# One 2048-column transposing DMA for q and k of a token block in the first chunk, and scores held behind the first gate/up step

## The chip, the cores and the metric

The kernel runs on one core of a Trainium2 chip. The metric is the device time of one execution in microseconds (us). The kernel before took 567.59 us, the median of three runs between 567.03 and 569.25 us. All views of the profile come from one profiled execution.

## The reference

The input x has 2048 tokens of 576 numbers, in bf16. The output is x plus the product of a windowed attention and a gated feed-forward block, both on the normalised x:

```
xn = layernorm(x)
q, k, v = split(xn @ wqkv)                 # 32 heads of 18 numbers
p = softmax(q k^T / sqrt(18), masked to the last 256 tokens)
s = (p v) @ wo
h = sigmoid(xn @ w_gate) * (xn @ w_up)     # 4608 columns each
out = x + s * silu(h @ w_down)
```

## The kernel before

**Tiles and stages.** The tokens are worked in four chunks of 512 (CH), each of four blocks of 128 (P). A chunk goes through the layernorm, q, k and v for each block (line 465), the attention, the gate and up products (line 810, called f below), the down product (line 930, called f2) and the output projection (line 740). The contraction over 576 is cut in nine pieces of 64 rows. In f, rows 0 to 63 of the TensorE array work on gate and rows 64 to 127 on up, so two matmuls of 64x512 run side by side; one tile of 128 columns (ft, 36 in a chunk) takes nine such pairs, 18 matmuls.

**An order written by a planner.** Every piece of work is an Op with an engine, a cost, dependencies and a priority. The function schedule() books them by start time on five in-order queues (PE, ACT, DVE, POOL, and SP for all DMAs), and emit() writes the queues out with semaphore waits. So the order on each queue is fixed when the kernel is built; on the chip, an instruction whose input is late holds all that stands behind it on its queue. DMAs are booked with an issue cost on SP, and with bytes on one shared transfer line of 320 bytes/ns.

**q and k.** For the scores, q and k must lie with their head rows on partitions. build_qk() copies the projection of one block out of PSUM into a buffer of 32 heads padded to 32 columns (1024 columns), q by DVE and k by ACT, and one transposing DMA (line 213, issued at 518) moves it to qkp. Chunk 0 issues eight of these: the first three from the ring pk, the other five from the first half of the five slots of expr, which the attention later uses for the exponentials. In qkp a head group holds 512 columns of q, 512 of k, and 256 of the keys that the chunk before left (the tail, copied by POOL at 641). In chunk 0 the eight DMAs are kept behind the weights of the third group of f (QKT_BEHIND, line 859).

**Scores.** build_unit() makes a unit: 16 or 24 small matmuls (line 594) into PSUM banks 0 to 3, two exponentials on ACT (612), masks on DVE (630). Four units serve a pair of head groups, and build_pv() (663) follows. Chunk 0 has 16 units. Units are put between steps of f, which is the filler; f uses banks 4 to 7, and its tiles end with a tanh on ACT (824) and a multiply on DVE (828).

**Weights of f.** Three tiles share a group of weights (fg), loaded by four DMAs into a ring of three slots (RW). Group 3 takes the slot of group 0, so its loads can start when tile 2 has been worked, and it is needed by tile 9.

**The exchange at XS.** Until tile XS[c], gate and up of a tile end in the same pair. At that tile two pieces of gate are worked in the upper rows, with weights from an extra load (sat, load_x()), and from there gate ends two pairs ahead of up. The last up tile takes the two places back. XS is 10 in chunk 0 and 1 in the others.

Of the kernel before, what the change touches and what calls it, by code (L numbers as in the profile page):

```python
# [4 lines left out]
ACTF = mybir.ActivationFunctionType  # L5
# [5 lines left out]
DH = 18  # L11
F = 4608
P = 128
CH = 512
# [23 lines left out]
RPK = 3  # L38
# [2 lines left out]
NOT = 4  # L41
WO_PRIO = 1
KL = 4 * DH
RS = 4
RXF = 2
RTH = 2
RREC = 2
RBN = 4
XS = (10, 1, 1, 1)
XP = (4, 0)  # L50
RUN = 3
WX_PRIO = -1
# [20 lines left out]
DMA_ISSUE_NS = 440.0  # L73
W_ISSUE_NS = 660.0
XT_ISSUE_NS = 1300.0
OC_SLACK = 3000.0
LATE_SLACK = 5000.0
LN_STEP = 1
XT_CUT = 4
QKT_BEHIND = {2: 0}  # L80
WARM = 10
X0_SLACK = 0.0
# [4 lines left out]
W_FACTOR = 1.42  # L87
X0_FACTOR = 1.7
XT_BYTES = 1.2
XT0_BYTES = 1.5  # L90
W0_FACTOR = 1.5
DMA_LAT_NS = 1600.0
DMA_BYTES_PER_NS = 320.0
# [80 lines left out]
class Builder:  # L174
# [141 lines left out]
    def build_init(self):  # L316
# [23 lines left out]
        self.op_pkz.append(op("ACT", 2500, lambda e: e.memzero(self.expr[:, :, 0:2, :]), "pkz2", prio=0))  # L340

    def warm(self, n, name, deps):
        ps = Psum((3,))
# [141 lines left out]
            "p t (h d) -> p t h d", d=DH)  # L485

    def build_qkv(self, c):
        self.op_q, self.op_k, self.op_qkt = [], [], []
        old = [o for l in self.op_sc[c - 1] for o in l] + self.op_tail if c > 0 else []
        order = QKV_FIRST if c == 0 else QKV_NEXT  # L490
        prev = None
        for w in order.split():
            i, j = int(w[1]), "qkv".index(w[0])
            o = (self.build_v if j == 2 else self.build_qk)(c, i, j, old)
            if c > 0:
                o.odeps += ([prev] if prev and QKV_CHAIN else []) + (self.op_xn[QKV_GATE] if not prev else []) + ([self.f2_ops[QKV_F2]] if QKV_F2 else [])
                o.prio = QKV_PRIO
            prev = o

    def build_qk(self, c, i, j, old):  # L500
        extra = len(self.op_qkt) - RPK if c == 0 else -1
        if extra < 0:
            spk, dpk = self.r_pk.take()
            pk = self.pk[:, spk, :, :]
        else:
            dpk = []
            pk = self.expr[:, extra, 0:2, :].rearrange("p a (h d) -> p (a h) d", d=HP)
        o, ps = self.project(c, i, j, f"qk:{c}:{i}:{j}", dpk, self.op_pv[c - 1][NHG - 1] if c > 0 else None)

        def f_ev(e):  # L510
            dst = pk[:, :, 0:DH].rearrange("p (t h) d -> p t h d", t=2)
            if j == 0:
                return e.tensor_copy(dst, self.halves(ps))  # L513
            return e.activation(dst, self.halves(ps), ACTF.Copy)
# [6 lines left out]
        if extra < 0:  # L521
            self.r_pk.release(spk, dm)
        else:
            self.r_exp.release(extra, dm)
        (self.op_q, self.op_k)[j].append(dm)
        self.op_qkt.append(dm)
        return o

# [49 lines left out]
    def build_unit(self, c, u, low, up, masks):  # L578
# [5 lines left out]
        def f_sc(e):  # L584
            for _, k in slots:
                for j in range(4):
                    r0 = 32 * j
                    for half, pieces in enumerate((low, up)):
                        if k >= len(pieces):
                            continue  # L590
                        hg, kb, q0, n, pos = pieces[k]
                        b = ps.banks[j] * 512 + pos * 64
                        k0 = CH + kb * 64 if kb >= 0 else 2 * CH + (kb + 4) * 64
                        r = e.matmul(self.ps[64 * half:64 * half + 64, b:b + n * 64],  # L594
                                     self.qkp[r0:r0 + DH, hg, k0:k0 + 64],
                                     self.qkp[r0:r0 + DH, hg, q0 * 64:(q0 + n) * 64],
                                     start=True, stop=True, tile_position=(r0, 64 * half))
            return r
# [174 lines left out]
    def build_ffn(self, c):  # L773
# [67 lines left out]
        for n0, n1 in zip(cuts, cuts[1:]):  # L841
# [60 lines left out]
            for key in done:  # L902
# [342 lines left out]
```

## Time and profile before

| what | value |
|---|---|
| median of three runs | 567.59 us (567.03 to 569.25) |
| the profiled execution, device time | 567.65 us |
| its span in the trace | 565.0 us |
| mean granted TensorE clock | 0.999 of full |
| TensorE matmul busy | 555.0 us (98%) |
| ACT busy / DVE busy | 274.6 us (49%) / 307.4 us (54%) |
| bytes moved by DMA | 73.29 MB, mean 130 GB/s |

The span runs from the first to the last instruction; the device time is 2.65 us longer. A busy TensorE (PE) is one with a matmul under way; the ends of matmuls are modelled. In the views, "x16" is a count of instructions merged in a row, the number in brackets is the idle time ahead of the first of them with what ended it, and "SPq" is the DMA-issuing queue. A wait for several semaphores is put down to the one that came last by the profile; where the engine named cannot be the cause, it was another, often a DMA.

### The profile page before, as it was taken

How to read it: one execution, taken by the hardware profiler on the slowest of the kernel's cores; microseconds unless marked ns; L12 is line 12 of the kernel's file. 1: busy time of each engine (PE TensorE's matmuls, PEld its weight loads, DVE VectorE, ACT ScalarE, POOL GpSimd, SP SyncE). 2: the span in 40 equal slices, each digit the busy share in tenths (PEclk: the TensorE clock that was granted, in tenths of full speed). 3: DMA queues.
4: the chain of work that ended last, by engine and by line, in shares of the span. 5: the costliest groups of instructions: out<-in, count | busy, mean ns of one | idle time of the engine just before them, and what ended most of it. 6: DMA issues, size and time to landing. Idle time of an engine off the chain costs nothing.

```text
span 565.0 us, 17870 instructions
## 1 busy us (share of the span) xinstructions
PE 555.0 (98%) x7830; PEld 283.0 (50%) x7854; DVE 307.4 (54%) x664; ACT 274.6 (49%) x372; POOL 28.2 (5%) x55
## 2 busy tenths in 40 slices
PE   8999999999999999999999999999999999999997
PEld 5634444457544444456654444445665444444544
DVE  6136987741136886772204778767121586686213
ACT  7456665514146947721407576580220855855011
POOL 3000001010000100010000011001000000000100
PEclk9999999999999999999999999999999999999999
DMA  8999999628956665324794665713559355660001
GB/s 200 219 187 249 231 224 215 136 62 114 181 105 148 151 151 135 86 52 83 106 210 109 144 153 122 161 36 71 89 124 206 87 126 129 147 131 23 20 22 43
DMA packets 126026, 73.29 MB, mean 130 GB/s; under 512 B 54782, under 2 KB 125438, under 8 KB 125950
## 3 DMA queue, kind: packets, MB, share of 16 engines
q1 hardware_dynamic: 125950, 72.16, 62.0%
q8 instruction: 62, 1.02, 0.8%
q14 instruction: 14, 0.11, 0.1%
HBM read 55.48 MB, written 2.36 MB: 102 GB/s over the span
## 4 chain that ended last, share of the span: by engine, by line
PE 94%; SPq 2%; DMA 1%; issue 1%; DVE 1%; ACT 0%
PE ps L810 50%; PE ps L930 23%; PE ps L465 8%; PE ps L594 5%; PE ps L663 4%; PE ps L740 3%; SPq L214 2%; PE ps L960 2%; DMA wqkv_sb<-in_A_wqkv_dram 1%; ACT sat L755 0%; ACT expr L612 0%; DVE tf L679 0%; DVE hT L828 0%; DVE pk L681 0%; DVE tf L684 0%
## 5 line engine op out<-in xcount | busy, mean ns | idle before, releaser
L810 PE MATMUL ps<-xn,wgs 64*128 64x512 bf16 x2576 | 296.3, 377 | 1.4 <-ACT expr L612 1.4
L810 PEld LDWEIGHTS ps<-xn,wgs 64*128 64x128 bf16 x2576 | 119.4, 94 | 143.7 <-issue 8.9
L612 ACT ACTIVATE expr<-ps 128x1024 bf16<-128x1024 f32 x152 | 147.2, 1022 | 26.3 <-PE ps L594 26.1
L930 PE MATMUL ps<-wd_sb,hT 128*128 128x64 bf16 (+1 forms) x1056 | 131.0, 284 | 2.2 <-issue 1.0
L824 ACT ACTIVATE tring<-ps 128x512 bf16<-128x512 f32 x144 | 86.3, 600 | 82.8 <-PE ps L810 80.6
L828 DVE SCALAR_TENSOR_TENSOR hT<-tring,ps 128x512 bf16<-128x512 bf16 x144 | 97.9, 680 | 30.6 <-ACT tring L824 14.2
L930 PEld LDWEIGHTS ps<-wd_sb,hT 128*128 128x128 bf16 x1080 | 68.1, 98 | 65.0 <-issue 1.4
L630 DVE TENSOR_TENSOR expr<-expr,m 128x512 bf16<-128x512 bf16 (+2 forms) x152 | 58.5, 412 | 55.5 <-ACT expr L612 54.5
L991 ACT ACTIVATE thf<-ps 128x576 bf16<-128x576 f32 (+2 forms) x17 | 10.6, 622 | 135.5 <-PE ps L930 128.3
L993 DVE SCALAR_TENSOR_TENSOR thf<-thf,ps 128x576 bf16<-128x576 bf16 (+2 forms) x17 | 12.2, 719 | 106.5 <-ACT thf L991 106.5
L465 PE MATMUL ps<-wqkv_sb,xn 64*128 64x288 bf16 x864 | 54.7, 283 | 0.5 <-ACT xn L454 0.2
L465 PEld LDWEIGHTS ps<-wqkv_sb,xn 64*128 64x128 bf16 x864 | 42.9, 94 | 11.2 <-issue 1.8
L594 PEld LDWEIGHTS ps<-qkp 18*64 18x64 bf16 x1472 | 16.2, 103 | 32.6 <-ACT expr L612 14.0
L594 PE MATMUL ps<-qkp 18*64 18x320 bf16 (+4 forms) x1472 | 32.4, 259 | 0.1
L641 POOL COPY qkp<-qkp 128x256 bf16<-128x256 bf16 x24 | 9.8, 410 | 288.1 <-PE ps L594 288.1
L513 DVE CAST pk<-ps 128x576 bf16<-128x576 f32 x15 | 11.3, 755 | 23.1 <-PE ps L465 22.9
L703 DVE STREAM_TRANSPOSE op__63<-pk 128x512 bf16<-128x512 bf16 x32 | 22.3, 698 | 0.2
L663 PEld LDWEIGHTS ps<-expr,vau 64*32 64x32 bf16 x1440 | 18.0, 92 | 7.6 <-issue 4.9
L681 DVE STREAM_TRANSPOSE pk<-ps 128x512 f32<-128x512 f32 x32 | 21.5, 673 | 0.0
L663 PE MATMUL ps<-expr,vau 64*32 64x320 bf16 (+5 forms) x1440 | 20.9, 253 | 0.3
L740 PE MATMUL ps<-wo_sb,oT 64*128 64x512 bf16 (+1 forms) x288 | 18.7, 283 | 0.1
L679 DVE STREAM_TRANSPOSE tf<-ps 128x512 f32<-128x512 f32 x16 | 11.5, 716 | 11.8 <-PE ps L663 11.8
(54 smaller groups left out, 197.1 us busy)
## 6 DMA issues: line engine op xcount, KB each, us to landing
wgs<-in_B_w_gate_dram SPq DMA_DIRECT2D x48, 240.0 KB, 3.9
wgs<-in_B_w_up_dram SPq DMA_DIRECT2D x48, 240.0 KB, 4.9
wgs<-in_B_w_up_dram SPq DMA_DIRECT2D x48, 192.0 KB, 4.0
wgs<-in_B_w_gate_dram SPq DMA_DIRECT2D x48, 192.0 KB, 4.8
wd_sb<-in_B_w_down_dram SPq DMA_DIRECT2D x9, 576.0 KB, 8.2
xf<-in_A_x_dram SPq DMA_DIRECT2D x18, 144.0 KB, 2.2
out_dram<-xf SPq DMA_DIRECT2D x15, 144.0 KB, 2.0
xr<-in_A_x_dram SPq DMA_DIRECT2D x14, 144.0 KB, 4.7
```

The costliest lines, as they stand in the source:

```text
L465: r = e.matmul(self.bank(ps, HV, hf), self.xn[r0:r0 + 64, k, i * P:(i + 1) * P], self.wqkv_sb[r0:r0 + 64, j, k, :], start=(k == 0), stop=( ...
L594: r = e.matmul(self.ps[64 * half:64 * half + 64, b:b + n * 64], self.qkp[r0:r0 + DH, hg, k0:k0 + 64], self.qkp[r0:r0 + DH, hg, q0 * 64:(q0 ...
L612: return e.activation(self.expr[:, es, 2 * pr:2 * pr + 2, :], src, ACTF.Exp, scale=SM_SCALE)
L630: return e.tensor_tensor(ap, ap, m, ALU.mult)
L663: r = e.matmul(self.ps[32 * j:32 * j + 32, b + q0 * 64:b + (q0 + n) * 64], vf[:, v0:v0 + 32], self.expr[p0:p0 + 64, es, j, pos * 64:(pos + ...
L681: t3 = self.rd("DVE", dve_ns(CH), lambda e, tg=tg, hg=hg: e.transpose(tg, self.bank(ps2[hg][1])), f"t3:{c}:{hg}", deps=[o, self.last_mul] ...
L703: t2 = self.op("DVE", dve_ns(CH), lambda e, on=on: e.transpose(self.op_[:, hg % NOT, :], on.rearrange("p g d -> p (g d)")), f"t2:{c}:{hg}" ...
L740: r = e.matmul(self.bank(ps2[w], n1 - n0, n), self.oT[r0:r0 + 64, kt, qi * P:(qi + 1) * P], self.wo_sb[r0:r0 + 64, kt, n0:n1], start=(swap ...
L810: return e.matmul(self.bank((pg, pu)[gu][ft]), w, self.xn[r0:r0 + 64, i, :], start=first, stop=last, tile_position=(r0, 0))
L824: return e.activation(self.tring[:, st_, :], self.bank(ps), ACTF.Tanh, scale=0.5)
L828: return e.scalar_tensor_tensor(self.hT[:, ft, :], self.tring[:, st_, :], 1.0, self.bank(ps), ALU.add, ALU.mult)
L930: r = e.matmul(self.ps[:, b + n0:b + n1], lhsT, self.wd_sb[:, q, fl, n0:n1], start=(ft == 0), stop=(ft == NFT - 1))
```

## The change

In chunk 0, q and k of a block are laid side by side in one buffer of 2048 columns (the slots 0 and 1 of pk for block 0, all four rows of the slots 0 to 2 of expr for the others), with the head groups of q and k alternating. One transposing DMA moves both, so there are four instead of eight; each waits for both copies. To let one DMA write both, q and k stand at one stride in qkp (KO = 640 columns): 512 of q and 128 of the tail, then 512 of k and the other 128 of the tail. The addresses of the scores and of the tail copy follow. The memset of expr covers 3 slots whole instead of 5 slots half. Chunks 1 to 3 keep their eight DMAs of 1024 columns, at the new addresses.

The planner's costs change for these DMAs: 1500 ns of issue for 2048 columns (1300 for 1024 before), and a factor of 1.2 on the bytes where it was 1.5. XS of chunk 0 goes from 10 to 13. In chunks 1 to 3 every score unit is ordered behind the first step of f (SC_GATE).

```diff
+KO = CH + P
-XS = (10, 1, 1, 1)
+XS = (13, 1, 1, 1)
+XT0_ISSUE_NS = 1500.0
+SC_GATE = 0
-XT0_BYTES = 1.5
+XT0_BYTES = 1.2
...
-        self.op_pkz.append(op("ACT", 2500, lambda e: e.memzero(self.expr[:, :, 0:2, :]), "pkz2", prio=0))
+        self.op_pkz.append(op("ACT", 2500, lambda e: e.memzero(self.expr[:, 0:3, :, :]), "pkz2", prio=0))
...
     def build_qk(self, c, i, j, old):
-        extra = len(self.op_qkt) - RPK if c == 0 else -1
-        if extra < 0:
+        if c == 0:
+            both = self.pk[:, 0:2, :, :].rearrange("p j h d -> p (j h d)") if i == 0 else \
+                self.expr[:, i - 1, :, :].rearrange("p a c -> p (a c)")
+            pk = both.rearrange("p (t g j h d) -> p t g j h d", t=2, g=4, j=2, d=HP)[:, :, :, j, :, 0:DH]
+            dpk = []
+        else:
             spk, dpk = self.r_pk.take()
             pk = self.pk[:, spk, :, :]
-        else:
-            dpk = []
-            pk = self.expr[:, extra, 0:2, :].rearrange("p a (h d) -> p (a h) d", d=HP)
...
-        c0 = j * CH + i * P
-        dm = self.dma(self.qkp[:, :, c0:c0 + P], pk.rearrange("p h d -> p (h d)"),
-                      (XT_BYTES if c else XT0_BYTES) * 8 * P * P * 2, f"qkt:{c}:{i}:{j}", ("qk", i, j), deps=[ev] + old, prio=0,
-                      issue=XT_ISSUE_NS, transpose=True)
+        if c == 0:
+            if j == 0:
+                self.op_qe.append(ev)
+                return o
+            dst = self.qkp[:, :, :].rearrange("p g (j c) -> p (g j) c", j=2)[:, :, i * P:(i + 1) * P]
+            dm = self.dma(dst, both, 2 * XT0_BYTES * 8 * P * P * 2, f"qkt:{c}:{i}", ("qk", i), deps=[ev, self.op_qe[i]] + old,
+                          prio=0, issue=XT0_ISSUE_NS, transpose=True)
...
+        else:
+            c0 = j * KO + i * P
+            dm = self.dma(self.qkp[:, :, c0:c0 + P], pk.rearrange("p h d -> p (h d)"), XT_BYTES * 8 * P * P * 2,
+                          f"qkt:{c}:{i}:{j}", ("qk", i, j), deps=[ev] + old, prio=0, issue=XT_ISSUE_NS, transpose=True)
...
-                        k0 = CH + kb * 64 if kb >= 0 else 2 * CH + (kb + 4) * 64
+                        k0 = KO + kb * 64 if kb >= 0 else CH + (kb + 4) // 2 * KO + kb % 2 * 64
...
-                    self.qkp[:, hg, 2 * CH:2 * CH + 2 * P], self.qkp[:, hg, 2 * CH - 2 * P:2 * CH]),
+                    self.qkp[:, hg, :].rearrange("p (j c) -> p j c", j=2)[:, :, CH:CH + P],
+                    self.qkp[:, hg, KO + CH - 2 * P:KO + CH].rearrange("p (j c) -> p j c", j=2)),
...
             prev = o
+            if n0 == SC_GATE and c > 0:
+                for l in self.op_sc[c]:
+                    for u in l:
+                        u.odeps.append(o)
```

More of the change, by code (lines that the diff above doesn't have):

```diff
@@ L487, in build_qkv @@
     def build_qkv(self, c):
-        self.op_q, self.op_k, self.op_qkt = [], [], []
+        self.op_q, self.op_k, self.op_qkt, self.op_qe = [], [], [], []
         old = [o for l in self.op_sc[c - 1] for o in l] + self.op_tail if c > 0 else []
@@ L508, in build_qk @@
         o, ps = self.project(c, i, j, f"qk:{c}:{i}:{j}", dpk, self.op_pv[c - 1][NHG - 1] if c > 0 else None)
         def f_ev(e):
-            dst = pk[:, :, 0:DH].rearrange("p (t h) d -> p t h d", t=2)
+            src = self.halves(ps)
+            if c == 0:
+                dst, src = pk, src.rearrange("p t (g h) d -> p t g h d", g=4)
+            else:
+                dst = pk[:, :, 0:DH].rearrange("p (t h) d -> p t h d", t=2)
             if j == 0:
-                return e.tensor_copy(dst, self.halves(ps))
@@ L514, in f_ev @@
-            return e.activation(dst, self.halves(ps), ACTF.Copy)
+                return e.tensor_copy(dst, src)
+            return e.activation(dst, src, ACTF.Copy)
         ev = self.rd("ACT" if j else "DVE", act_ns(D) if j else dve_ns(D), f_ev, f"qke:{c}:{i}:{j}",
                      deps=[o, self.op_pkz] + [t for t in (self.op_on[c - 1] if c > 0 else [])], prio=1, psum=[ps])
-        c0 = j * CH + i * P
-        dm = self.dma(self.qkp[:, :, c0:c0 + P], pk.rearrange("p h d -> p (h d)"),
-                      (XT_BYTES if c else XT0_BYTES) * 8 * P * P * 2, f"qkt:{c}:{i}:{j}", ("qk", i, j), deps=[ev] + old, prio=0,
-                      issue=XT_ISSUE_NS, transpose=True)
@@ L521, in build_qk @@
-        if extra < 0:
+        if c == 0:
+            if j == 0:
[4 more added lines that the diff above has]
+                          prio=0, issue=XT0_ISSUE_NS, transpose=True)
+            if i > 0:
+                self.r_exp.release(i - 1, dm)
+            else:
+                for k in (0, 1):
+                    self.r_pk.rel[k].append(dm)
+            self.op_q.append(dm)
+            self.op_k.append(dm)
+        else:
+            c0 = j * KO + i * P
+            dm = self.dma(self.qkp[:, :, c0:c0 + P], pk.rearrange("p h d -> p (h d)"), XT_BYTES * 8 * P * P * 2,
+                          f"qkt:{c}:{i}:{j}", ("qk", i, j), deps=[ev] + old, prio=0, issue=XT_ISSUE_NS, transpose=True)
@@ L522, in build_qk @@
             self.r_pk.release(spk, dm)
-        else:
-            self.r_exp.release(extra, dm)
-        (self.op_q, self.op_k)[j].append(dm)
+            (self.op_q, self.op_k)[j].append(dm)
         self.op_qkt.append(dm)
```

## The prediction

> **What bounds the kernel now.** I read the page first, then the waits of PE, then PE's, SP's and ACT's timelines of the first 50 us, then the landings of single DMAs, and last the score matmuls by stage.
>
> ```profile
> PE 555.0 (98%) x7830; PEld 283.0 (50%) x7854; DVE 307.4 (54%) x664; ACT 274.6 (49%) x372; POOL 28.2 (5%) x55
> ...
> PE 94%; SPq 2%; DMA 1%; issue 1%; DVE 1%; ACT 0%
> ```
>
> PE has a matmul under way for 555.0 of 565.0 us, and the chain that ended last runs through PE for 94%. The change removes no matmul. So it can win only from the 10 us in which PE stands still, or lose by adding to them. The waits say where these are:
>
> ```profile
> PE ps L347 <- DVE neghalf L318: 1.5, 1, 1.5
> PE ps L810 <- ACT expr L612: 1.4, 1, 1.4
> PE ps L930 <- issue: 1.0, 6, 0.2
> PE ps L444 <- DVE xnr L421: 0.9, 1, 0.9
> ```
>
> The first and fourth are the start, ahead of anything the change touches; the third is six pieces of under 0.2 us. The second is one stall of f, and it lies in chunk 0:
>
> ```profile
> 17.83 1.24 PE L810 MATMUL ps<-xn,wgs 64*128 64x512 bf16 x10
> ...
> 23.70 12.75 PE L810 MATMUL ps<-xn,wgs 64*128 64x512 bf16 x116
> 36.55 0.42 PE L594 MATMUL ps<-qkp 18*64 18x320 bf16 x16
> 36.90 3.19 PE L810 MATMUL ps<-xn,wgs 64*128 64x512 bf16 x28
> 40.03 0.43 PE L594 MATMUL ps<-qkp 18*64 18x64 bf16 x24
> 40.39 1.04 PE L810 MATMUL ps<-xn,wgs 64*128 64x512 bf16 x8
> 42.79 1.04 PE L810 MATMUL ps<-xn,wgs 64*128 64x512 bf16 x8 [1.37 <-ACT expr L612]
> ```
>
> Count the matmuls of f up to the stall: 10 + 116 + 28 + 8 = 162 = 9 x 18. PE stands exactly ahead of tile 9, the first tile of weight group 3. The profile names the exponentials, but f does not read them. So I look for the weights on SP:
>
> ```profile
> 19.67 0.62 SPq L214 DMA_DIRECT2D wgs<-in_B_w_up_dram  x1
> 20.33 7.47 SPq L213 DMA_TRANSPOSE qkp<-pk  x3
> 27.85 7.86 SPq L213 DMA_TRANSPOSE qkp<-expr  x5
> 35.76 0.60 SPq L214 DMA_DIRECT2D wgs<-in_B_w_gate_dram  x1
> 36.40 0.63 SPq L214 DMA_DIRECT2D wgs<-in_B_w_up_dram  x1
> 37.07 0.62 SPq L214 DMA_DIRECT2D wgs<-in_B_w_gate_dram  x1
> 37.73 0.62 SPq L214 DMA_DIRECT2D wgs<-in_B_w_up_dram  x1
> ```
>
> The eight transposing DMAs hold SP from 20.33 to 35.71, and the four loads of group 3 stand behind them. The slot they go to is free much earlier, when tile 2 ends: 54 matmuls, 10 of them done early, so 23.70 + 44 x 12.75/116 = 28.5 us. The last of the four, issued at 37.73, takes this long to land:
>
> ```profile
> L214 SPq DMA_DIRECT2D wgs<-in_B_w_up_dram x1: 616/616/616, 37.7 to 37.7; - x1
> ...
> DMA to landing us min/median/max: 4.7/4.7/4.7
> ```
>
> It lands at 42.4, and PE goes on at 42.79. Could it be a PSUM bank that ACT frees late? ACT's timeline rules that out:
>
> ```profile
> 39.06 0.60 ACT L824 ACTIVATE tring<-ps 128x512 bf16<-128x512 f32 x1
> 40.60 1.94 ACT L612 ACTIVATE expr<-ps 128x1024 bf16<-128x1024 f32 x2 [0.94 <-PE ps L594]
> 42.42 0.60 ACT L824 ACTIVATE tring<-ps 128x512 bf16<-128x512 f32 x1
> ```
>
> Tile 9 takes the banks of tile 7, whose tanh ended at 39.66. The next one, for tile 8, ends at 43.02, after PE had gone on. So the stall is weights late behind the transposing DMAs, and it is worth 1.37 us.
>
> **The change, part by part.**
>
> **The DMAs.** Eight issues become four, of twice the columns. No row shows 2048 columns. Smaller ones are there:
>
> ```profile
> L213 SPq DMA_TRANSPOSE xn<-xnr x24: 1209/1271/2224, 105.8 to 397.6; - x24
> L213 SPq DMA_TRANSPOSE qkp<-pk x27: 1232/1336/3429, 20.3 to 428.7; - x27
> ```
>
> The xn group has 640 and 512 columns (576 in the mean), the qkp group 1024. From 576 to 1024 columns the median grows by 0.065 us; carried on in a straight line, 2048 columns take 1.336 + 0.065 x 1024/448 = 1.48 us (the lower bound). In proportion to the columns they take 2 x 1.336 = 2.67 us (the upper bound). I take 1.5 us, by the nearer pair of rows, which are almost flat.
>
> The Trainium skill speaks against this: "DMA: Bandwidth & Descriptors", in a table of its section "Why a DMA increments its semaphore by 16 and not by 1", gives 262,144 cycles of issue for an SBUF to SBUF transpose of 8,192 tiles on generations before trn3, one push for each tile. By that, twice the columns cost twice the issue, and nothing would be saved; the two rows above do not follow it between 576 and 1024 columns, and it stays as a rival below.
>
> Part of the 15.38 us on SP isn't issue: 8 x 1.34 is 10.7, and the rest, 4.7 us, is blocking, which shows in the first and second DMA:
>
> ```profile
> L213 SPq DMA_TRANSPOSE qkp<-pk x1: 3370/3370/3370, 20.3 to 20.3; - x1
> ...
> DMA to landing us min/median/max: 7.3/7.3/7.3
> ...
> L213 SPq DMA_TRANSPOSE qkp<-pk x1: 2697/2697/2697, 23.8 to 23.8; - x1
> ...
> DMA to landing us min/median/max: 4.7/4.7/4.7
> ...
> L213 SPq DMA_TRANSPOSE qkp<-expr x1: 2282/2282/2282, 33.4 to 33.4; - x1
> ...
> DMA to landing us min/median/max: 4.2/4.2/4.2
> ```
>
> These landed at 27.6, 28.5 and 37.6. The weights ahead of them still fill the DMA engines then, and that stays. What limits the new ones from below is the data: the closest two landings are 0.9 us apart for 1024 columns. From 27.6 for the first 1024 columns the other seven need at least 6.3 us, so the last DMA lands no earlier than 33.9; if nothing is won, at 37.6 as now. SP was free 1.9 us ahead of that landing (35.7), so it will be free between 32.0 and 35.7. My value is about 32.5: four issues of 1.5 are 6 us, so data and the old blocking set the end.
>
> **The wait added.** A block's DMA now waits for q and k. The copies of k come last:
>
> ```profile
> 20.61 0.65 ACT L514 ACTIVATE expr<-ps 128x576 bf16<-128x576 f32 x1 [3.02 <-PE ps L465]
> ...
> 23.92 0.65 ACT L514 ACTIVATE expr<-ps 128x576 bf16<-128x576 f32 x1 [0.45 <-PE ps L465]
> ```
>
> The first is done at 21.26, 0.93 us after SP gets there; all are done at 24.57. Behind the waiting DMA stand the other three and then group 3. This costs nothing while the first DMA would be blocked by the weights until 23.7 anyway; without that cover it is 0.93 us on SP.
>
> **The loads behind.** Group 3 landed 42.4 - 35.7 = 6.7 us after SP came free. So it lands at 39.2 (bounds 38.7 to 42.4). PE needs it at 41.43. The stall is gone if SP is free by 34.7, that is, 1.0 us earlier than now: gain 1.37 us. Later groups follow the same queue and are earlier too.
>
> **The first score.** With 16 matmuls (four pieces for four heads) it is the unit of keys 2 to 5, which needs q and k of blocks 1 to 3, so it waited for the seventh of eight DMAs before (k of block 2) and waits for the last of four now. The planner books 262,144 bytes x 1.5 / 320 = 1.23 us a DMA before, 1.97 us now; seven are 8.6, four 7.9 us. So it places the first score some 0.7 us sooner, near 35.8. The data, at 33.9 to 37.6, may be up to 1.9 us late there; I take zero, as my value of SP free at 32.5 puts the landing at 34.4. Starting attention earlier wins nothing by itself, as f fills PE meanwhile.
>
> **XS from 10 to 13.** Tiles 10 to 12 lose the lead of two pairs (2 x 0.22 us), so their tanh starts 0.2 to 0.4 us later. The cover is the second pair of banks, a whole tile of 2 us. Bounds: nothing, and 0.4 us for each of three tiles where an exponential stands ahead of the tanh, 1.2 us. I take nothing, since the planner sees this wait and puts scores elsewhere.
>
> **Memset, copies, scores, tail.** The memset of expr grows from 5 x 1024 to 3 x 2048 columns, by a fifth:
>
> ```profile
> 3.48 2.32 ACT L340 ACTIVATE expr<-expr 128x2560 uint32<-128x2560 uint32 x1
> 6.48 3.37 ACT L454 ACTIVATE xn<-ps 128x512 bf16<-128x512 bf16 x6 [0.68 <-PE ps L444]
> ```
>
> That is 0.46 us of the 0.68 that ACT waits next; without this cover it would delay the first copy of xn by 0.46. The other instructions keep their sizes.
>
> **SC_GATE.** In chunk 1 the order is so already (columns of the stretches: PE busy with scores and their count, then weight loads):
>
> ```profile
> 124.66:160.20 35.54, 0.00 (x0) 0.00 (x0) 1.00 0.88 149
> 160.20:245.00 84.80, 8.53 (x384) 4.14 (x384) 1.00 0.51 116
> ...
> 160.21 1.25 PE L810 MATMUL ps<-xn,wgs 64*128 64x512 bf16 x9
> ```
>
> No score matmul stands ahead of the first step of f at 160.21. It costs nothing where the order stays.
>
> **Sum.** Span 565.0 - 1.37 = 563.6; with the 2.65 us around the span, 566.3 against 567.65 of the profiled execution. That execution is 0.06 above the median, so **566.2** against 567.59, 0.24% less.
>
> **The rivals.** A measurement of this kernel can tell 0.5% (2.8 us) from no change.
>
> *No gain at the stall.* If the profile is right to name the exponentials, or SP is free only after 34.7 by other work moved up, the time stays at 567.6. For it: the second exponential ends at 42.54, close to 42.79. Against it: the count of 162.
>
> *Issue in proportion to columns.* Four DMAs of 2.67 us with the same blocking: last landing 37.6 as now, group 3 at 42.4. PE stands at the first score from 35.8 to 37.7, 1.9 us, and reaches tile 9 at 43.3, after the weights: 1.9 - 1.4 = +0.5, 568.1. For it: the second and later DMAs of a run (1.336) are slower than the first (1.232), as if each waited for the one ahead. Against it: 576 columns take 1.271. The page's rule of a push for each tile leads here.
>
> *Slower: 2048 columns block SP.* If a DMA of 2048 columns is too much for the queue to take ahead, each blocks as the first did, 3.37 + 1.37 = 4.7 us. Then SP is free at 21.3 + 19 = 40.3, the last DMA lands at 42.2, and the first score holds PE for 6.4 us, less the 1.4 of the old stall: 567.6 + 5.0 = 572.6. It decides from a landing later than 35.8 + 1.4 + 2.8 = 40.0. For it: 3.37 and 2.28 us. Against it: the five in between go at 1.34.
>
> *More than the stall.* The short waits of f2 (1.0) and the one of the first transposes on PE (L444, 0.9) go too: 566.2 - 1.9 = 564.3. Nothing in the change reaches them, but a plan that is made anew may.
>
> **How the numbers follow.** Forecast 0.64, no gain 0.08, proportion 0.16, blocking 0.08, more 0.04. Faster than 564.7 is the last and 0.01 of the forecast's edge: 0.05. Slower than 570.4 is blocking and 0.01 of proportion with the exchange's 1.2 on top: 0.09. The rest, 0.86, lies within 0.5%. The range goes from 565.0 (1.2 under the forecast: the short waits of f2, or twice the 0.56 by which the lowest of the three runs lies under the median) to 568.6 (proportion, with 0.5 of the exchange); it leaves out the last two cases and the edges.
>
> **What would show it.** Right: four transposing DMAs on SP of about 1.5 us plus blocking, the loads of group 3 issued by 34.7, no wait of PE ahead of its matmul 163 of f, a first score without a wait, and PE's other waits as before. Wrong: issues near 2.7 us or more, a PE wait ahead of the first score matmul, or a wait ahead of tiles 10 to 14.

## The result, and the profile after

The kernel after took 567.22 us, the median of 22 runs (566.27 to 568.96); the kernel before, in 22 runs beside it, 568.54 us (566.21 to 569.89). The ratio is 0.998, with a 95% interval of 0.9971 to 0.999. So the change makes the kernel about 0.2% faster, and 22 executions of each are enough to tell that.

The profiled execution of after took 568.96 us, with a span of 566.8. It is the slowest of its 22, and its span is 1.8 us longer than that of the profiled execution of before. Setting the two spans against each other would give the wrong sign. Where the extra time lies can be seen in the trace. First the page, then PE's longest waits:

```profile
PE 558.1 (98%) x7854; PEld 282.9 (50%) x7854; DVE 308.5 (54%) x664; ACT 275.0 (49%) x372; POOL 28.3 (5%) x55
```

```profile
PE ps L683 <- issue: 1.9, 1, 1.9
...
PE ps L613 <- DMA qkp<-expr: 0.9, 1, 0.9
```

PE is as full as before. (24 matmul records are missing from the trace of before, so the two busy times can't be compared to the microsecond.) The stall of f is not among the waits of this execution. In its place stands 0.9 us ahead of a score (line 613 is 594 of before) for the transposing DMA. The longest wait is new as well: 1.9 us ahead of the second PV, with no releaser that the profile shows. PE's timeline places them (start, duration, what, and in brackets the wait ahead of it):

```profile
23.95 12.75 PE L830 MATMUL ps<-xn,wgs 64*128 64x512 bf16 x116
37.55 0.43 PE L613 MATMUL ps<-qkp 18*64 18x64 bf16 x24 [0.85 <-DMA qkp<-expr]
37.92 3.20 PE L830 MATMUL ps<-xn,wgs 64*128 64x512 bf16 x28
...
41.40 3.16 PE L830 MATMUL ps<-xn,wgs 64*128 64x512 bf16 x26
...
45.12 2.12 PE L830 MATMUL ps<-xn,wgs 64*128 64x512 bf16 x18 [0.21 <-DVE hT L848]
...
75.75 0.35 PE L683 MATMUL ps<-expr,vau 64*32 64x192 bf16 x17 [1.86 <-issue]
```

The first score stands behind 126 matmuls of f, in the same place as before. Tile 9 begins eight matmuls into the piece at 41.40, near 42.3, without a wait; before, PE went on there at 42.79. Two more profiles of after (below) have 0.2 and 0.4 us at the second PV, so 1.86 belongs to this execution and not to the change. (In the profile of before the same PV is one row of 1.52 us, in two others of before one of 1.11.) Now SP, and the landing of the last transposing DMA:

```profile
19.86 0.62 SPq L217 DMA_DIRECT2D wgs<-in_B_w_up_dram  x1
21.54 5.45 SPq L216 DMA_TRANSPOSE qkp<-pk  x1
27.09 8.16 SPq L216 DMA_TRANSPOSE qkp<-expr  x3
35.30 0.60 SPq L217 DMA_DIRECT2D wgs<-in_B_w_gate_dram  x1
...
37.27 0.62 SPq L217 DMA_DIRECT2D wgs<-in_B_w_up_dram  x1
```

```profile
L216 SPq DMA_TRANSPOSE qkp<-expr x1: 3272/3272/3272, 32.0 to 32.0; - x1
...
DMA to landing us min/median/max: 5.4/5.4/5.4
```

Four issues hold SP for 13.7 us, where eight held it for 15.4. They start 1.2 us later, because the first waits for the copy of k, so SP comes free at 35.25 instead of 35.71. The last landing is 32.0 + 5.4 = 37.4, against 37.6 before. In this execution the data arrive as late as ever.

Part of that is a pause. While SP stands in its last issue, the DMA engines move next to nothing for 1.5 us (stretch, its length, busy time and count of PE, PEld, DVE, ACT, POOL, then granted clock, DMA share, GB/s):

```profile
34.00:34.50 0.50, 0.50 (x8) 0.24 (x6) 0.18 (x1) 0.00 (x0) 0.00 (x0) 1.00 0.39 3
34.50:35.00 0.50, 0.50 (x8) 0.19 (x4) 0.00 (x0) 0.20 (x1) 0.00 (x0) 1.00 0.06 6
35.00:35.50 0.50, 0.50 (x8) 0.23 (x6) 0.07 (x1) 0.40 (x1) 0.00 (x0) 1.00 0.08 9
```

The profile of before has the same, with 8 GB/s between 34.0 and 35.0. It shows in the landings: one gap is 4.16 us in after and 2.99 in before, and behind it the next landing follows by 1.69 and 0.88. Where nothing pauses, landings are 1.3 to 1.4 us apart for 1024 columns (before) and 2.44 to 2.54 for 2048 (the three profiles of after). Ahead of the pause, at 33.3 us in after and 33.6 in before, a transfer of 16 KB begins on the profile's instruction queue (q8). No run moves that transfer, so it is not shown to be the cause.

In chunks 1 to 3 nothing changed: from the start of the q, k, v work to that of the next chunk both kernels take 138.27 us for chunk 1 and 138.18 for chunk 2, and from the start of chunk 3 to the end 164.0 and 164.1 us.

### The profile page after: what moved, and what is told of

Read it like the earlier page. It is cut to its first block, busy times and chain, and to the rows that moved or that the text cites. A ratio compares the mean times of both kernels' runs of the same rounds, so it can differ in the third digit from the quotient of the medians.

```text
span 566.8 us, 17897 instructions
## 1 busy us (share of the span) xinstructions
PE 558.1 (98%) x7854; PEld 282.9 (50%) x7854; DVE 308.5 (54%) x664; ACT 275.0 (49%) x372; POOL 28.3 (5%) x55
## 3 DMA queue, kind: packets, MB, share of 16 engines
q8 instruction: 62, 1.02, 0.8%
## 4 chain that ended last, share of the span: by engine, by line
PE 94%; SPq 2%; DMA 2%; issue 1%; DVE 0%; ACT 0%
PE ps L830 50%; PE ps L954 23%; PE ps L468 8%; PE ps L613 5%; PE ps L683 4%; PE ps L760 3%; SPq L217 2%; PE ps L984 2%; DMA wqkv_sb<-in_A_wqkv_dram 1%; DMA qkp<-expr 1%; ACT expr L631 0%; DVE hT L848 0%; DVE expr L649 0%; DVE thf L1017 0%; ACT thf L1015 0%
## 5 line engine op out<-in xcount | busy, mean ns | idle before, releaser
L954 PE MATMUL ps<-wd_sb,hT 128*128 128x512 bf16 (+1 forms) x1080 | 133.7, 286 | 0.0
L954 PEld LDWEIGHTS ps<-wd_sb,hT 128*128 128x128 bf16 x1080 | 68.3, 98 | 64.9 <-issue 1.4
L1015 ACT ACTIVATE thf<-ps 128x576 bf16<-128x576 f32 (+2 forms) x17 | 10.6, 623 | 134.3 <-PE ps L954 127.1
L613 PEld LDWEIGHTS ps<-qkp 18*64 18x64 bf16 x1472 | 16.2, 103 | 33.4 <-ACT expr L631 14.0
L521 DVE CAST pk<-ps 128x576 bf16<-128x576 f32 x13 | 9.8, 754 | 21.5 <-PE ps L468 21.5
```

Of the source, the lines that this page charges most:

```text
L954: r = e.matmul(self.ps[:, b + n0:b + n1], lhsT, self.wd_sb[:, q, fl, n0:n1], start=(ft == 0), stop=(ft == NFT - 1))
```

## The experiments

The ratio stands for each against the kernel before in the same set of runs. The kernel before had medians of 568.79, 568.69 and 568.0 us in three sets (29 runs each) and 568.42 in a fourth (27).

**The two kernels once more** (`before_again`, `after_again`, and in another set `before_third`, `after_third`; no edit). They give more profiles and the noise of the comparison.

> The kernel before, profiled once more. Stall theory: the one wait of PE in f lies again ahead of tile 9, of 1.0 to 1.6 us, because SP holds the loads of weight group 3 behind the eight transposing DMAs until 35.7 us. Code theory (a rival for the 1.3 us between the two medians): the time varies by 1 to 3 us between executions through waits of PE in the second PV of chunk 0 that nothing in the profile explains, and this trace shows another length there than the 0.4 us of the first. Time: as before, ratio 1.000.

> The changed kernel, profiled once more. Stall theory: SP is free at about 35.2 us again, 0.5 earlier than before, no wait ahead of tile 9, and a wait of 0.7 to 1.0 us ahead of the first score in its place; ratio 0.998 to 0.999. Code theory: the wait of 1.9 us in the second PV has another length here or is absent, and the ratio of 0.998 comes from this wait being shorter on the mean than in the kernel before.

> The kernel before, profiled a third time in this study's calls. Stall theory: one wait ahead of tile 9 of 1.3 to 1.9 us, with the clock at half for 3 us behind it where the wait is over 1.5 us. Ratio 1.000.

> The changed kernel, profiled a third time, for the spread of its waits. Stall theory in its new form (data hold SP, the plan only places the wait): the waits of PE ahead of the first score and ahead of tile 9 sum to 0.8 to 1.2 us, none of them long enough for the granted clock to drop; the wait in the second PV is anything from 0 to 1.9. Ratio 0.998 to 0.9995.

Before: 568.21 us, 0.9991 (0.9975 to 1.0007), and 568.54 us, 1.0006 (0.9993 to 1.002). After: 567.78 us, 0.9994 (0.9977 to 1.0011), and 567.68 us, 0.9989 (0.9975 to 1.0002). Neither of these two ratios of after is clear of 1. With the first comparison the three, weighted by their intervals, give about 0.9985 (0.9978 to 0.9992), some 0.85 us. PE's timelines around tile 9, first of after_again, then of after_third:

```profile
36.69 0.43 PE L613 MATMUL ps<-qkp 18*64 18x64 bf16 x24 [0.26 <-DMA qkp<-expr]
...
42.33 2.12 PE L830 MATMUL ps<-xn,wgs 64*128 64x512 bf16 x18 [0.76 <-DMA wgs<-in_B_w_up_dram]
```

```profile
36.65 0.43 PE L613 MATMUL ps<-qkp 18*64 18x64 bf16 x24
...
42.24 2.12 PE L830 MATMUL ps<-xn,wgs 64*128 64x512 bf16 x18 [0.71 <-DMA wgs<-in_B_w_up_dram]
```

Here the profile itself names the weights as what ends the wait of tile 9. SP is free early in both, at 33.86 and 33.97, but that brings the weights hardly sooner. SP and the last load of group 3 in after_again:

```profile
33.91 0.79 SPq L217 DMA_DIRECT2D wgs<-in_B_w_gate_dram  x1
```

```profile
L217 SPq DMA_DIRECT2D wgs<-in_B_w_up_dram x1: 1120/1120/1120, 36.1 to 36.1; - x1
...
DMA to landing us min/median/max: 5.9/5.9/5.9
```

It lands at 42.0 (after_third: 41.9; after: 42.1; before: 42.4, and 42.6 to 42.8 in three more profiles). In three profiles of after the waits at the first score and at tile 9 sum to 0.85, 1.02 and 0.71 us, 0.86 in the mean. The other profiles of before show more at tile 9, and put it down to another engine each time:

```profile
43.13 1.89 PE L810 MATMUL ps<-xn,wgs 64*128 64x512 bf16 x8 [1.86 <-ACT tring L824]
```

```profile
42.96 1.04 PE L810 MATMUL ps<-xn,wgs 64*128 64x512 bf16 x8 [2.04 <-DVE expr L630]
```

With 1.37 of the first and 1.32 of the run with extra transposes below, the mean is 1.65 us. The difference, 0.79 us, is close to the measured gain of 0.85, though it comes from three and four executions. After the first of these waits (before_again) eight matmuls took 1.89 us instead of 1.04. The stretches show why (columns as above):

```profile
42.00:43.00 1.00, 0.00 (x0) 0.00 (x0) 0.59 (x2) 0.86 (x2) 0.00 (x0) 0.97 1.12 217
43.00:44.00 1.00, 0.87 (x6) 0.40 (x8) 0.92 (x3) 0.00 (x0) 0.00 (x0) 0.50 1.14 229
```

The granted clock is 0.50 for some 3 us. After the 2.04 us of before_third it stays at 1.00. Both stretches have a DMA share above 1.1: the DMA engines are busy throughout.

**The 2048 columns cut in two** (`a_split`, and the same again in another set, `a_split_again`; after, with every other instruction in its place on the queues):

```diff
+        o.fn = lambda e, d=dst[:, 0:8, :], s=both[:, 0:1024]: e.dma_start_transpose(d, s)
+        n = Op("SP", 0, lambda e, d=dst[:, 8:16, :], s=both[:, 1024:2048]: e.dma_start_transpose(d, s),
...
+        sp.insert(sp.index(o) + 1, n)
```

> The changed kernel with the order of every queue kept, and each of its four DMAs of 2048 columns issued as two of 1024 in the same place: the new plan without the new DMAs. Data theory (the transposing DMAs move some 1024 columns in 1.35 us whatever their number, so SP is held by data and not by issues): SP is free at 34 to 36 us as with four DMAs, the first score and tile 9 wait 0.8 to 1.5 us together as in the changed kernel, ratio to the changed kernel 0.999 to 1.001. Issue theory (the prediction's): twice the issues hold SP 4 us longer, to 38 or later, tile 9 waits 3 us or more, 568.8 or above.

> The kernel after with each DMA of 2048 columns issued as two of 1024, once more. Theory A (the plan brings the gain, the halved number of DMAs nothing): ratio near 0.9985, as after. Theory B (the halved number of DMAs brings it): ratio near 1.000, with a first score wait of 1.5 us or more; the two runs together tell 0.0015 apart only just.

568.24 us, 0.9993 (0.9975 to 1.0012), and 569.42 us, 1.0017 (0.9999 to 1.0036). SP and PE of a_split:

```profile
32.43 1.34 SPq L1237 DMA_TRANSPOSE qkp<-expr  x1
33.82 0.60 SPq L217 DMA_DIRECT2D wgs<-in_B_w_gate_dram  x1
```

```profile
37.76 0.43 PE L613 MATMUL ps<-qkp 18*64 18x64 bf16 x24 [1.76 <-DMA qkp<-expr]
38.12 4.88 PE L830 MATMUL ps<-xn,wgs 64*128 64x512 bf16 x28
```

and PE of a_split_again:

```profile
37.24 0.43 PE L613 MATMUL ps<-qkp 18*64 18x64 bf16 x24 [0.75 <-DMA qkp<-expr]
```

With eight issues again SP comes free at 33.8 and 34.0, as early as with four: 35.25, 33.86 and 33.97 in three profiles of after, and only in the first of these does the pause fall within SP's issues. So halving the issues does not free SP sooner. But the last landings are 37.6 and 37.1, against 37.4, 36.6 and 36.5 of after, and the first score waits 1.26 us in the mean against 0.37. Together the two ratios give 1.0005 (0.9992 to 1.0018), that is 0.0020 above after, with an interval of 0.0015 to either side: in this order of the queues the DMAs of 2048 columns bring about 1.1 us, and only just more than the noise. The landings explain part of it at most: 2048 columns take 2.5 us where two DMAs of 1024 take 2.7, and in both profiles of a_split the pause (a gap of 3.2 us) falls on one of the last two landings. After the 1.76 us wait of a_split the granted clock fell to half as well, and 28 matmuls took 4.88 us instead of 3.20.

**The plan without the DMAs of 2048 columns** (both from before, planned anew, with the scores of chunks 1 to 3 held behind the first step of f, where they stand in the order of before already). `b_xs13g` moves the exchange; `b_plan` also books the DMAs of chunk 0 as after does:

```diff
-XS = (10, 1, 1, 1)
+XS = (13, 1, 1, 1)
```

> The kernel before with the exchange of chunk 0 at tile 13 instead of 10 and with the scores of chunks 1 to 3 held behind the first step of f; the eight DMAs and their costs stay. Theory A (the gain of the kernel after comes from the new place of the exchange and the plan it makes): ratio near 0.9985, wait ahead of tile 9 as before or shorter. Theory B (the gain comes from the DMAs that are free earlier): ratio 1.000 within 0.0015, with a wait of 1.3 to 2.0 us ahead of tile 9.

```diff
-XS = (10, 1, 1, 1)
+XS = (13, 1, 1, 1)
...
-XT0_BYTES = 1.5
+XT0_BYTES = 1.2
```

> As the run above, and with the bytes of the eight DMAs of chunk 0 booked at a factor of 1.2 instead of 1.5, so the plan is near that of the kernel after, with eight DMAs of 1024 columns. Its first score stands behind 118 matmuls of f instead of 126, 0.9 us sooner. Theory A: ratio near 0.9985. Theory B: the last landing stays at 37.0 to 37.6 us, so PE waits about 1.5 us ahead of the first score and little or nothing ahead of tile 9; ratio 1.000 within 0.0015.

b_xs13g: 570.21 us, 1.0046 (1.0026 to 1.0066). b_plan: 577.56 us, 1.0161 (1.0138 to 1.0185). Neither theory had losses of this size. PE of b_xs13g, then of b_plan:

```profile
43.61 1.26 PE L810 MATMUL ps<-xn,wgs 64*128 64x512 bf16 x10 [1.64 <-ACT tring L824]
```

```profile
35.38 0.42 PE L594 MATMUL ps<-qkp 18*64 18x320 bf16 x16
...
140.10 2.34 PE L465 MATMUL ps<-wqkv_sb,xn 64*128 64x288 bf16 x18 [6.77 <-DMA qkp<-pk]
```

The exchange at 13 leaves the stall of tile 9 where it was, with old DMAs. In b_plan the first score stands 0.9 us sooner and finds its data there: the wait of 1.5 us that I expected did not come. Its landings show no pause (the q8 transfer begins at 37.5, behind the last of them, at 35.9). And then chunk 1 has an order in which PE waits 6.77 us. So the plan alone is not the gain.

**The transposes by themselves** (`b_micro`; before, with seven extra transposing DMAs in chunk 3, where f no longer loads weights: four of 1024 columns, then, when these have landed, three of 2048. They move old exponentials over old q and k that nothing reads.)

```diff
+    jobs = [(b.qkp[:, :, c:c + P], b.expr[:, k, 0:2, :].rearrange("p a c -> p (a c)")) for k, c in enumerate((512, 1152, 384, 1024))]
+    jobs += [(q2[:, :, i * P:(i + 1) * P], b.expr[:, i, :, :].rearrange("p a c -> p (a c)")) for i in range(3)]
...
+    sp[at:at] = new
```

> The kernel before with seven more transposing DMAs on SP in chunk 3, behind the transfers to the output projection, where the DMA engines are nearly idle: four of 1024 columns one behind the other, then, once the last has landed, three of 2048. They move old exponentials over old q and k, which nothing reads. Issue theory: a 2048 issue takes 1.4 to 1.6 us. Proportion: 2.6 to 2.8. Data theory: the first 2048 issue is short (1.4 to 1.8 us), the later ones are held to the pace at which 2048 columns move, 2.6 to 2.8 us, and landings of 2048 come 2.6 to 2.8 us apart, those of 1024 1.3 to 1.4.

The first and last of the 1024s, then the first and last of the 2048s (issue in ns, start, and time from issue to landing):

```profile
L1213 SPq DMA_TRANSPOSE qkp<-expr x1: 1285/1285/1285, 530.3 to 530.3; - x1
...
DMA to landing us min/median/max: 3.3/3.3/3.3
...
L1213 SPq DMA_TRANSPOSE qkp<-expr x1: 1340/1340/1340, 534.4 to 534.4; - x1
...
DMA to landing us min/median/max: 3.3/3.3/3.3
...
L1213 SPq DMA_TRANSPOSE qkp<-expr x1: 1868/1868/1868, 537.7 to 537.7; - x1
...
DMA to landing us min/median/max: 5.3/5.3/5.3
...
L1213 SPq DMA_TRANSPOSE qkp<-expr x1: 1990/1990/1990, 543.5 to 543.5; - x1
...
DMA to landing us min/median/max: 4.4/4.4/4.4
```

One execution was taken, 567.72 us. The 1024s land from 533.6 to 537.7, 1.36 us apart, which for 262,144 bytes is 193 GB/s. They are issued 1.35 us apart, so this cannot tell whether the data or the issue sets the pace. The first 2048 columns are issued in 1.87 us, not 2.67, but the second issue then stands 3.85 us. The three 2048s take 10.2 us from the first issue to the last landing (537.7 to 547.9); six 1024s at that pace would take 3.3 + 5 x 1.36 = 10.1. But among the 2048s there is a pause as in chunk 0 (6 GB/s between 540.5 and 541.0, a q8 transfer from 539.6), and among the 1024s none. So the run does not show that 2048 columns are as slow as two times 1024; by after's landings without a pause (2.5 us) they are a little faster.

**Two transposing DMAs put behind the weights** (`b_g3first`; before, planned anew):

```diff
-QKT_BEHIND = {2: 0}
+QKT_BEHIND = {2: 0, 3: 6}
```

> The kernel before, with only the last two transposing DMAs moved behind the four loads of weight group 3 on SP. Stall theory: the wait of 1.37 us ahead of tile 9 goes and no other comes, scores start about 4 us later, which costs nothing as f fills PE: 1.0 to 1.5 us less, ratio 0.9975 to 0.9985. Rival, that the exponentials and not the weights end this wait: the wait moves with the scores, ratio 1.000. Rival, that the start of the attention counts: slower by 1 us or more.

571.66 us, 1.0052 (1.0028 to 1.0076). PE:

```profile
41.29 0.42 PE L594 MATMUL ps<-qkp 18*64 18x320 bf16 x16
...
101.78 3.17 PE L810 MATMUL ps<-xn,wgs 64*128 64x512 bf16 x14 [3.63 <-DMA wgs<-in_B_w_up_dram]
```

Group 3 was issued from 32.06 and tile 9 began without a wait, so the weights behind the transposing DMAs were the cause of the stall. But the kernel lost 2.9 us: the first score came 4.7 us later, and the last group of weights, issued at 90.42, took 11.1 us to land. PE stood 3.63 us for it, and the granted clock was 0.50 from 99.4 until about 106. Whether the late scores cost something beside this late load was not separated.

**Tile 9's weights first** (`b_t9` and, the same again, `b_t9_again` of before, `a_t9` of after; the four loads of group 3 become eight, the 128 columns of tile 9 ahead of the rest, all in the same place on SP):

```diff
+    for k, (first, rest) in enumerate(zip(parts(0, P), parts(P, FG * P))):
...
+        o.fn = lambda e, d=first[0], s=first[1]: e.dma_start(d, s)
+        n = Op("SP", 0, lambda e, d=rest[0], s=rest[1]: e.dma_start(d, s), f"w9:{k}", o.deps, 0, lane=("w9", k))
...
+        if u.name.startswith("f:0:") and 10 <= int(u.name.split(":")[2]) <= 11:
+            u.add_dep(new)
```

> The kernel before with the order of every queue kept, and the four loads of weight group 3 cut in two: first the columns of tile 9 (a third), then those of tiles 10 and 11. Weights theory: the first four land 1 to 3 us sooner, the wait ahead of tile 9 (1.37 and 1.86 us in two traces) falls under 0.3, the granted clock has no drop behind it, and the time falls by 1.2 to 2 us, ratio 0.9965 to 0.998, more than the change itself brought. Rival, that the exponentials or a bank end this wait: it stays, ratio 1.000. Rival, that four more issues on SP make group 4 late: a wait of 1 us or more ahead of tile 12.

> The changed kernel with the same cut of the loads of group 3. Weights theory: its wait ahead of tile 9 (0 and 0.76 us in two traces) goes, the one ahead of the first score (0.85 and 0.26) stays: 0.3 to 0.8 us less than the changed kernel, ratio to before 0.9965 to 0.9985, and no faster than the kernel before with that cut by more than 0.3 us. If the new DMAs have a worth of their own beside the stall, this one is faster than the kernel before with the cut by 0.5 us or more.

> The kernel before with the 128 columns of tile 9 loaded ahead of the rest of group 3, once more. Theory A (a wait that is taken away at 42 us comes back at the last group of weights): again no wait ahead of tile 9, again 1 to 3 us near 98 us with the last load taking about 10 us, ratio 1.000 within 0.0015. Theory B (the late load at 98 us was of that one execution): no wait near 98 us, a span shorter by 1.3 to 2.0 us than with the wait, ratio near 0.997.

b_t9: 568.34 us, 1.0006 (0.9991 to 1.0022). b_t9_again: 569.04 us, 1.0005 (0.999 to 1.002). a_t9: 568.84 us, 1.0013 (0.9997 to 1.0029). The wait ahead of tile 9 is gone in all three, and none is faster. Both runs of before together give 1.0005, with 0.0011 to either side, where the wait that went is 0.0029 of the time. PE of b_t9, and the last load that it waits for there:

```profile
100.19 2.12 PE L810 MATMUL ps<-xn,wgs 64*128 64x512 bf16 x18 [2.04 <-ACT tring L824]
```

```profile
L214 SPq DMA_DIRECT2D wgs<-in_B_w_up_dram x1: 617/617/617, 89.9 to 89.9; - x1
...
DMA to landing us min/median/max: 10.0/10.0/10.0
```

The load lands at 99.9 and PE goes on at 100.19. In the profile of before the same load took 6.0 us from 90.3 and was there at 96.3, ahead of PE. I took this for the rule: what is won at 42 us is lost at 98. The second profile contradicts it. Its last load lands within 7.8 us and PE has no wait near 98; instead it waits 0.81 us at the first score, 0.15 to 0.30 at 44 us, 0.87 at 64 and 0.39 at 72:

```profile
37.92 0.42 PE L594 MATMUL ps<-qkp 18*64 18x320 bf16 x16 [0.81 <-DMA qkp<-expr]
```

That the gain does not arrive is measured twice; where it goes differs from one execution to the next. In a_t9 the profiled execution waits 0.72 us at the first score, 0.4 for weights at 70 us and 1.17 at the second PV.

**The plan's costs and places.** Three edits of after, each planned anew:

```diff
-XT0_BYTES = 1.2
+XT0_BYTES = 1.35
```

> The changed kernel with the planner's factor on the bytes of these four DMAs at 1.35 instead of 1.2, which puts the first score 10 matmuls (1.1 us) later in PE's order. Theory one, that the wait of 0.85 us at the first score only covers the weights of group 3, which land at 42.1 in any case: the wait at the score goes, and one of 0.5 to 0.9 us comes back ahead of tile 9; ratio to the changed kernel 0.999 to 1.001. Theory two, that the wait at the score is a cost of its own: 0.8 us less than the changed kernel.

578.01 us, 1.0166 (1.014 to 1.0193). The first score comes 10 matmuls later and no longer waits, and 0.83 us appears ahead of tile 9. But the new plan also moved work in chunk 1, where PE stands 6.76 us for a transposing DMA:

```profile
140.30 2.34 PE L468 MATMUL ps<-wqkv_sb,xn 64*128 64x288 bf16 x18 [6.76 <-DMA qkp<-pk]
```

```diff
-XS = (13, 1, 1, 1)
+XS = (10, 1, 1, 1)
```

> The changed kernel with the exchange of gate pieces back at tile 10, planned anew. If XS = 13 matters by itself (tiles 10 to 12 without the lead), this one is faster by up to 1.2 us; if it only serves the plan, the waits of PE fall in other places and the ratio to before is 0.998 to 1.002, with the difference made of waits that the trace names outside tiles 10 to 12.

569.37 us, 1.0031 (1.0003 to 1.0059), against 0.9989 with 13 in the same set. Its profile has 0.95 us ahead of the first score and a wait for the last group of weights:

```profile
99.51 0.61 PE L830 MATMUL ps<-xn,wgs 64*128 64x512 bf16 x4 [0.95 <-DVE expr L649]
```

The last load of that group was issued at 88.66 and landed 10.6 us later, at 99.3.

```diff
-            if n0 == SC_GATE and c > 0:
+            if False:
```

> The changed kernel without SC_GATE, planned anew. The prediction held that the gate costs and brings nothing because scores stand behind the first step of f anyway. Rival: without it the planner puts scores of chunk 1 among the last steps of f2, which changes PE's mode more often and moves later work; chunk 1 then takes more than 138.3 us, and the kernel is slower by 0.3 to 2 us, ratio 0.9985 to 1.002.

573.97 us, 1.0101 (1.008 to 1.0122). Without the gate the scores of chunk 1 stand among the steps of f2 (L954), ahead of the first step of f (at 164.15):

```profile
124.53 11.20 PE L468 MATMUL ps<-wqkv_sb,xn 64*128 64x288 bf16 x180
...
147.41 0.42 PE L613 MATMUL ps<-qkp 18*64 18x320 bf16 x16
...
162.55 0.43 PE L613 MATMUL ps<-qkp 18*64 18x320 bf16 x24 [1.93 <-DMA qkp<-pk]
...
267.19 2.99 PE L468 MATMUL ps<-wqkv_sb,xn 64*128 64x288 bf16 x46
```

Chunk 1 takes 267.19 - 124.53 = 142.66 us instead of 138.27.

No variant was measurably faster than after.

## Where the prediction held, and where it failed

Sign and size came out: I forecast 0.24% less, and 0.2% less was measured, at 567.22 us within my own range for it. That the size came out is luck in part. I took 1.37 us off, the whole stall; the first comparison has 1.32, all three together 0.85, and it is a larger stall of which half stayed. What also failed is the claim that a measurement of this kernel can tell only 0.5% from no change. With 22 executions of each the interval is 0.1% to either side, and a chance of 0.05 for a gain beyond a bound of 0.5% said little about whether a gain would be seen.

- **The step that failed: SP free at 32.5 by four issues of 1.5 us, and the weights of group 3 6.7 us behind that.** SP came free at 35.25, 33.86 and 33.97. In the last two that is ahead of the 34.7 at which I had the stall gone. Yet group 3 landed at 42.0 and 41.9, which is 8.1 and 7.9 us after SP came free, and PE still waited 0.76 and 0.71 us ahead of tile 9. So 6.7 us was not a fixed delay, and a free SP alone was not what the weights lacked. (In b_g3first, with two transposing DMAs moved behind them, they were issued from 32.06 and landed at 39.1.) They landed 0.3 to 0.5 us earlier than the 42.4 of the profile of before, where I had 3.2. What they waited for instead, in a stretch in which the last transposes, a pause and the loads of group 4 share the DMA engines, stays open.
- **The stall: right in cause.** The count of 162 matmuls pointed to the weights of group 3 behind the transposing DMAs, against the engine that the profile named. Moving them ahead (b_g3first) or only tile 9's part of them (b_t9) took the wait away, and in two profiles of after the profile names them.
- **The size of the first term: 1.37 where about 0.8 came.** It was mis-sized from two sides. The stall was larger than the one profile showed (1.65 us in the mean of four), and 0.86 us of it stays, at the first score or at tile 9.
- **The 2048 columns at 1.5 us of issue: failed.** The first that the weights do not block is issued in 1.75 to 1.83 us in the three profiles of after (1.87 in b_micro), nearer to my lower bound than to the upper. But the next one is then held for 2.8 to 2.95 us, and the DMAs land 2.5 us apart where nothing pauses, nearly in proportion to the 1.36 of 1024 columns. I took 0.9 us for 1024 columns from the closest pair of landings. That pair came in a burst behind a hold-up, and such bursts (0.82 to 0.96 us) are in every other profile with eight DMAs too; a row of DMAs does not keep that pace. Since the bytes can go faster than the row, the row's pace may be one of issuing and not of data; no run separates the two. The last landing was 36.5 to 37.4 instead of 34.4.
- **"The weights ahead of them still fill the DMA engines": right for two DMAs of three.** The last weights ahead landed at 26.7. The DMA issued at 33.4, held for 2.28 us, had none ahead of it; the pause from 34.0 was there.
- **The rival "in proportion to columns" came close in the pace and not in the price.** It had 2.67 us for 2048 columns, the last landing at 37.6 and a wait of 1.9 us at the first score, net +0.5. The first score did not move up by the planner's 0.7 us: it stands behind the same 126 matmuls, is reached near 36.6 and not 35.8, and so waits 0.85, 0.26 and 0 us. My own value for this wait, zero, was too low in two of three.
- **The Trainium skill's rule of a push for each tile**, which I weighed there, would double the issue. The first issue of a row does not follow it (from 1.34 to 1.87 us), the row nearly does (from 1.36 to 2.5 us between landings). "Advanced Engine Details and Errata" of the Trainium skill, in "X-Bar Transpose (TRN2)", expects 350 to 400 GB/s of such a transfer. By that, as an estimate, 1024 columns would land 0.66 to 0.75 us apart and my pace of 0.9 would have been safe. Measured were 193 GB/s in the row of b_micro and at most 320 between two landings in a burst, and the measurement decides.
- **The wait for both copies: mis-sized.** I hid 0.93 us under the blocking by the weights. SP began at 21.54 instead of 20.33, then the first DMA blocked for 5.45 us and landed at 29.1, where the first two of before had landed by 28.5. Half a microsecond of it was not hidden.
- **The rival "2048 columns block SP": fell.** Only the first DMA holds SP so long (5.45 us); the others hold it for 1.75, 2.95 and 3.27, and it is free by 35.3, not 40.3.
- **XS at nothing: failed.** With the new DMAs 13 is worth some 2.4 us against 10 (0.9989 and 1.0031, intervals that just miss each other); with the old DMAs it loses (b_xs13g, 1.0046). I looked at the tanh of tiles 10 to 12; what differs is the order that the planner makes around the exchange, and which part of that order counts was not tried. I had costed the edits one by one and added them up, and here neither part wins alone.
- **SC_GATE at nothing: failed, for a reason that I had seen.** "It costs nothing where the order stays" was argued from the order before. Without the gate the plan of after has another order, and the gate is worth 573.97 - 567.68 = 6.3 us. It is not a gain of the change over before; it keeps a loss out that the other edits would have brought.
- **The memset: right.** 2.75 us instead of 2.32, and ACT's wait behind it shrank from 0.68 to 0.20 us.

Where did the rest of the expected gain go? Into the wait at the first score and what stays at tile 9. Both are waits for bytes, and from 36 us on the DMA engines are busy throughout (share of 1.11, 1.12 and 1.06 between 36, 56, 72 and 80 us in after). The last q and k land 0.2 to 1.1 us earlier than the 37.6 in the profile of before, not 3.2.

Four things stay open. What makes the DMA engines pause for some 1.5 us near 34 us, and what part of the gain is where the pause falls. Why the same last load of weights takes 6 us in some executions and 10 to 11 in those of b_t9, b_g3first and a_xs10. Which part of a new order costs PE 6.8 us in chunk 1 in a_b135 and b_plan: a transposing DMA is late there, but the reason was not followed further. And the wait without a releaser at the second PV, 0.2 to 1.9 us between executions of the same kernel; in after a q8 transfer begins at 73.0, ahead of it, but the cause was not tried.

## What to carry to other kernels

Before you count on fewer, larger DMAs, take the pace of a long row of landings (here 1.36 us for 1024 columns) and not the closest pair, and look at each landing, because a mean can hold a pause of 1.5 us. Where that pace accounts for the time that the queue is held, joining DMAs frees little. Do not carry over the delay from a free queue to a landing: here it grew from 6.7 to 8.1 us when the queue came free earlier. A stall in a stage whose DMA engines are busy can be worth less than its length, because PE then waits for another transfer; half of it came here, and none when the stall alone was taken away. And where an order is planned from costs, edits cannot be priced one by one: the place of the exchange, the gate and the booked bytes, each set without its partners, cost 0.3 to 1.6%, several times the gain of all the edits together.

## What was not expected of the hardware

- Transposing DMAs of 1024 columns on 128 partitions, issued in a row, land 1.36 us apart (193 GB/s), and those of 2048 columns 2.5 us apart (210 GB/s), so twice the columns in one DMA save about a tenth. In a burst behind a hold-up, 1024 columns follow by 0.82 to 0.96 us.
- In the same stretch the DMA engines stand nearly still for some 1.5 us (3 to 9 GB/s in after), half a microsecond after a 16 KB transfer began on the instruction queue. It is seen in profiles and was not caused on purpose.
- PE's granted clock fell to 0.50 for 3.4 us at a wait of 1.86 us (before_again), one of 1.76 us (a_split) and one of 1.93 us (a_nogate), and did not after 2.04 us (before_third) nor after 1.86 us at the second PV of after. "TensorE: Matmul & The Clock Gate" of the Trainium skill, in "What's actually happening", gives an idle window of about 3.4 us for that fall, and says that the window runs freely; the falls here came after a little over half of it, so the length of a wait alone does not say whether it costs more than itself.
